# The values' products of two steps in one visit, in the last steps of an attention and MLP kernel

## The chip, the core and the metric

The kernel runs on one core of one Trainium2 chip. The metric is the device time of one execution in microseconds; three runs are shown by their median and their extremes. A profile was taken of one further execution: it has records of every instruction on the engines (PE for TensorE's matmuls, PEld for its weight loads, DVE for VectorE, ACT for ScalarE, POOL for GpSimd) and of the DMAs.

## The reference

An adaLN block over 2048 positions of width 512: attention with 32 heads of 16, then a dense layer to 1792, Mish, and a dense layer back.

```python
h = _layernorm(x) * (1 + ca) + sa
qkv = (h @ wqkv).reshape(B, S, 3, H, Dh)           # H = 32, Dh = 16
p = _softmax(einsum("bhqd,bhkd->bhqk", q, k) * Dh ** -0.5)
x = x + ga * (einsum("bhqk,bhkd->bhqd", p, v) @ wo)
h = _layernorm(x) * (1 + cb) + sb
x = x + gb * (mish(h @ w1 + b1) @ w2)              # all in float32
```

## The kernel before, in words

**Head groups and steps.** Attention is cut into 32 head groups `n`: four blocks of 512 queries (`qb`) times eight groups of four heads. A head group takes 16 steps, one for each 128 keys, so `T` is 512 steps, and the loop at the file's end calls `step(t)` one by one. Two steps, an even and an odd one, form a pair (`u`). In the even one PE makes the scores of the two heads that lie in rows 64 to 127, for two key chunks (four scores, `own`); in the odd one those of the two heads in rows 0 to 63. A score (L618) is a matmul with 64 rows by 512 queries into one of the `ring` banks of PSUM; ACT takes the exponential (L621) into a buffer `pr`. Each head has three or four such buffers.

**Maxima.** A softmax needs the maximum of every row ahead of its scores. DVE takes it, 20 steps (`PRO`) ahead of the scores, from a first pass of products (L569, L571). `tm = t + PRO`; from step 492 on `tm >= T`, and no maxima are left to make.

**The values' products.** `pv(t)` (L628 to L639) multiplies the exponentials of key chunk `t` with the values: four matmuls, one for each head, with 128 rows by 32 columns each, at four places of the array side by side, into the bank `acc`. In the trace each float32 matmul of this kind shows as two, so one `pv` shows as x8. I call it a visit, because scores and unit matmuls before and behind it use the array as two halves of 64 rows, and this one as four strips of 32 columns. `step(t)` calls `pv(t - 2)` once, at its end or, where the step has no unit matmuls and maxima are left, in its middle (`mid`).

**Units.** What is left over of PE beside the scores goes to the units: output projection, up and down matmuls of the MLP for the block of queries before. `next_part` takes up to eight matmuls of a unit for a pair of steps. `mm_half` runs each of them in two halves: in the even step with rows 0 to 63, beside the scores that use rows 64 to 127, and in the odd step the other way round. In the last 20 steps a part has six matmuls, and a whole unit of twelve takes two pairs. When its last half is issued, `cur["fin"]` empties the unit's only bank `ms` into SBUF: there DVE does it (L828 for an up unit, L1007 for a down unit), and the next unit writes to the same bank.

Both halves of a matmul write to one bank, and the two row halves must not do that at once. So the first half matmul of a step is made to wait for an instruction of the step before: after the last half of a part, `cur["want"]` is set, the step's fourth score is issued, and that score's exponential on ACT is kept in `cur["after"]`.

```python
        i = nc.tensor.matmul(acc, l[64 * g:64 * g + 64], r[64 * g:64 * g + 64], start=start and not then, stop=bool(stop and then))
        if after is not None:
            tc.add_manual_dep(i.ins, after.ins.name,
...
                for m in beside[i]:
                    mm_half(m, second, cur.pop("after", None))
                if last:
                    cur["want"] = True
                    if i < len(mine):
                        emit(mine[i])
```

(The lines from `mm_half`, L129 on, and from `step`, L1397 on.)

**The last steps.** From step 494 on `first_part` adds two matmuls per step of the last block's output projection (shown as L134 `ring<-ka,o_hl`), for which one bank of the six in the ring is kept. A step then has four scores and two of these in one row half, six unit matmuls in the other. Behind step 511 come two calls with `pv` alone, and then `tail()`, the MLP of the last block of queries.

The order on each engine is the order in which this code emits the instructions.

Of the kernel before, what the change touches and what calls it, by code (L numbers as in the profile page):

```python
# [18 lines left out]
def adaln_block(ctx: ExitStack, tc: tile.TileContext, x, wqkv, wo, w1, b1, w2, c, w_mod, out):  # L19
# [13 lines left out]
    T = 16 * NIT  # L33
# [126 lines left out]
    def bank(tag="ms"):  # L160
        return ring() if tag == "ring" else ps.tile([P, TB], F32, tag=tag, name="bk", bufs=1)
# [413 lines left out]
    def max_pair(n, jq, kb):  # L575

        if n not in mxs:
            mxs[n] = ap.tile([P, 2, 8, 4], F32, tag="mx", name="mx", bufs=2)
        j, qs = divmod(jq, 4)
        kt, qt = ka[(2 * n + j) % NR], qa[(2 * n + j) % NR]  # L580
        pm = ring(2)
        for s in range(2):
            nc.tensor.matmul(pm[:, s, :], qt[64 * s:64 * s + 64, qs * P:(qs + 1) * P],  # L583
                             kt[64 * s:64 * s + 64, kb * TB:(kb + 1) * TB], start=True, stop=True)
        nc.vector.tensor_reduce(out=mxs[n][:, :, jq, kb:kb + 1], in_=pm, op=ALU.max, axis=AX.X)

    def neg_max(n):

        mx = mxs.pop(n)
        mm = ap.tile([P, 4, 2, 4], F32, tag="mm", name="mm", bufs=2)  # L590
        for v in range(2):
            nc.vector.tensor_reduce(out=mm[:, :, v, :], in_=mx.rearrange("p s (j q) k -> p (s j) q k", j=2), op=ALU.max,
                                    axis=AX.X)
        ats.setdefault(16 * n + 16 - PRO, []).append(lambda: max_rows(n, mm))
# [19 lines left out]
    def score(n, j, s, kc):  # L614
        def product():
            kt, qt = ka[(2 * n + j) % NR], qa[(2 * n + j) % NR]
            p_ = ring()
            nc.tensor.matmul(p_, kt[64 * s:64 * s + 64, kc * P:(kc + 1) * P], qt[64 * s:64 * s + 64, :],  # L618
                             start=True, stop=True)
            pr = ap.tile([P, TB], F32, tag=f"p{2 * j + s}", name="pr", bufs=3 + s)  # L620
            e = nc.scalar.activation(pr, p_, AF.Exp, scale=SCALE)  # L621
            pts[16 * n + kc, 2 * j + s] = pr
            return e
        return product
# [3 lines left out]
    def pv(t):  # L628
        if not 0 <= t < T:
            return  # L630
        n, kc = divmod(t, 16)
        if kc == 0:
            accs[n] = bank("acc")
        for h in range(4):
            o = (kc * 4 + h) * VW
            nc.tensor.matmul(accs[n][32 * h:32 * h + 32, :], vgs[n][:, o:o + 32], pts.pop((t, h)),  # L636
                             start=(kc == 0), stop=(kc == 15))
        if kc == 15:
            evac(n)  # L639
# [651 lines left out]
    def whole_units(h, credit):  # L1291

        cur["owed"] = cur.get("owed", 0) + credit
        while cur["owed"] > 0.49:
            if not cur["left"]:
                if not units or h < units[0][0]():
                    cur["owed"] = 0
                    return
                cur["tag"] = "acc" if cur.get("tag") == "ms" else "ms"
                cur["fin"] = units.pop(0)[1](cur["tag"])  # L1300
                cur["left"] = list(pe_queue)
                pe_queue.clear()
            m = cur["left"].pop(0)
            mm_go(m)
            cur["owed"] -= m[0].shape[-1] / TB
            if not cur["left"]:
                at(h + 1, lambda fin=cur["fin"]: fin(h + 1))
                cur["fin"] = None

    def maxima(n, u, s, others):  # L1310

        j, qs = divmod(u, 4)
        return ([max_tile(n, j, s, qs, kb) for kb in range(4 - others)],
                [max_tile(n, j, 1 - s, qs, kb) for kb in range(4 - others, 4)])

    def step(t):
        second = t % 2
        n, u = t // 16, t % 16 // 2
        tm = t + PRO
        run_hooks(2 * t)  # L1320
        if t < 0:

            for i in range(2):
                if tm < 16:
                    kb, jq = divmod(2 * tm + i, 8)
                else:
                    jq, kb = tm % 16 // 2, 2 * second + i
                max_pair(tm // 16, jq, kb)
            if second and tm % 16 == 15:
                neg_max(tm // 16)  # L1330
            run_hooks(2 * t + 1)
            for f in ats.pop(t, []):
                f()
            whole_units(2 * t + 1, CREDIT)
            do_specials(2 * t + 1)
            return
        s = 0 if second else 1
        own, others = ([score(n, j, v, 2 * u + i) for i in range(2) for j in range(2)] for v in (s, 1 - s))
        if not second and t < T:
            next_part(2 * t)  # L1340
        part = list(cur["part"])
        if not second:
            first_of["part"] = []
            if t == T - PRO:
                kept.append(NRING - 1)
            elif T - PRO < t < T:
                first_part(2 * t)
        f = len(part)
        if t >= T:
            if t == T:  # L1350
                cur["tag"] = "acc"
            run_hooks(2 * t + 1)
            pv(t - 2)
            whole_units(2 * t + 1, 8)
            do_specials(2 * t + 1)
            return
        if tm < T:
            o = max(0, (8 - f) // 2)
            mo, alone = maxima(tm // 16, tm % 16 // 2, s, o)

            mine = [x for p in zip(mo, own) for x in p] + own[len(mo):]
        else:
            o = max(0, (4 - f) // 2)
            mine = own[o:] if second else own[:4 - o]
            alone = others[4 - o:] if second else others[:o]

            if first_of["part"]:
                assert f
                for i, slot in enumerate(first_of["part"]):
                    mine.insert(2 + 2 * i, lambda slot=slot: [mm_half(m, 1 - second, None, second) for m in slot] and None)  # L1370
            m = len(mine)
            if f > m:
                mine = [mine[(i * m) // f] if (i + 1) * m // f > i * m // f else None for i in range(f)]
        beside = part + alone

        def emit(product):
            e = product()
            if e is not None and cur.pop("want", None):
                cur["after"] = e

        mid = False
        if cur.pop("new", None) and alone and len(mine) > f and t % 16 != 2:

            emit(mine.pop())
            emit(beside.pop())
        for i in range(max(len(mine), len(beside))):
            if i == len(mine) // 2:
                run_hooks(2 * t + 1)

            if not f and tm < T and i == (2 if mst.get("norming") else 3):  # L1390
                pv(t - 2)
                mid = True
            if i < f:
                last = i + 1 == f
                if i < len(mine) and mine[i] and not last:
# [7 lines that stand above are left out]
                    if second and not cur["left"]:  # L1403
                        cur["fin"](2 * t + 2)
                        cur["fin"] = None
            else:
                for x in (*mine[i:i + 1], *beside[i:i + 1]):
                    emit(x)
        if second and first_of["part"] and not first_of["left"]:
            first_of["fin"]()  # L1410
        if tm < T and tm % 16 == 15:
            neg_max(tm // 16)
        do_specials(2 * t + 1)
        if not mid:
            pv(t - 2)
        for f in ats.pop(t, []):
            f()

    def do_specials(h):
        if specials and h >= specials[0][0]():  # L1420
            fin = specials.pop(0)[1]()
            pe_run()
            at(h + 1, lambda: fin(h + 1))
# [116 lines left out]
    def run_hooks(h):  # L1540
        for f in hooks.pop(h, []):
            f()

    for t in range(-PRO, T + 2):
        step(t)
        prep_step(t)
    t = T + 2
# [32 lines left out]
```

## Time and profile before

| | |
|---|---|
| median of three runs | 1690.04 us (1687.92 to 1691.31) |
| the profiled execution | 1688.32 us, of which the span is 1686.5 |
| PE, ACT, DVE, POOL busy in the span | 1670.4, 1357.4, 1432.9, 812.5 us |
| steps 492 to 511, with the visit that ends them | 54.40 us, from 1530.80 to 1585.20 |
| the granted clock there | 1.00 |

A timeline row gives start, duration, engine, line, operation, what is written from what, shape and count; like instructions in a row are merged, and the duration is then that of all of them together. In brackets stands idle time ahead of it and what ended it. A matmul's duration reaches from its start to the end of its pipeline, so matmuls of one row half overlap, and the distance of their starts is what one costs.

### The profile page before, as it was taken

To read this page: it belongs to the slowest core of one execution; us is meant where nothing else is said; L and a number is where in the kernel's file an instruction comes from. 1 tells how busy PE (TensorE), PEld (TensorE's weight loads), DVE (VectorE), ACT (ScalarE), POOL (GpSimd) and SP (SyncE) were. 2 spreads that over 40 slices of the span, in tenths; PEclk is the share of its full clock that TensorE was granted. 3 is DMA by queue.
4 is the path that set the end of the run, shared out by engine and by line. 5 is a ranking of instruction groups with operands and counts; after the bars stand their busy time and mean duration, and the time that the engine had idled before them with its cause. 6 is when DMAs were issued, how large, how long until landed. Compare 5 with 4: busy or idle time off the path is not lost.

```text
span 1686.5 us, 33920 instructions
## 1 busy us (share of the span) xinstructions
PE 1670.4 (99%) x12491; PEld 924.4 (55%) x12491; DVE 1432.9 (85%) x2372; ACT 1357.4 (80%) x2612; POOL 812.5 (48%) x839
## 2 busy tenths in 40 slices
PE   8999999999999999999999999999999999999998
PEld 6755655555445455555555455555555455555687
DVE  6998888888999988888889888888889888883377
ACT  7257777777778988888878998888878988889674
POOL 5555224655313664556323565556323664555442
PEclk9999999999999999999999999999999999999999
DMA  8877656777755334434355434534344433534261
GB/s 261 264 251 188 157 145 197 205 228 218 225 136 161 97 93 104 120 81 130 82 137 161 106 77 98 139 80 122 100 133 120 130 93 81 149 97 135 76 227 63
DMA packets 114983, 239.00 MB, mean 142 GB/s; under 512 B 24500, under 2 KB 50120, under 8 KB 108864
## 3 DMA queue, kind: packets, MB, share of 16 engines
q1 hardware_dynamic: 114808, 236.82, 49.7%
q8 instruction: 99, 1.62, 0.4%
q14 instruction: 68, 0.56, 0.1%
q10 hardware_dynamic: 8, 0.00, 0.0%
HBM read 180.48 MB, written 51.45 MB: 138 GB/s over the span
## 4 chain that ended last, share of the span: by engine, by line
PE 92%; DVE 3%; ACT 2%; DMA 1%; issue 1%; POOL 0%; SPq 0%; ACTq 0%; DVEq 0%; POOLq 0%
PE bk L636 29%; PE ring L618 22%; PE ring L569 19%; PE bk L134 11%; PE bk L127 3%; PE ring L127 2%; PE ring L1249 2%; DVE mx L571 2%; ACT pr L621 1%; PE ring L583 1%; DMA qa<-mt 0%; PE ring L952 0%; PE ring L598 0%; DMA xt<-in_A_x 0%; PE ring L134 0%
## 5 line engine op out<-in xcount | busy, mean ns | idle before, releaser
L571 DVE TENSOR_REDUCE mx<-ring 128x1 f32<-128x512 f32 x1968 | 1221.9, 681 | 150.9 <-PE ring L569 136.2
L621 ACT ACTIVATE pr<-ring 128x512 f32<-128x512 f32 x2048 | 1078.7, 603 | 207.8 <-PE bk L134 116.3
L569 PE MATMUL ring<-ka,qa 64*128 64x512 f32 x1968 | 818.3, 429 | 1.3 <-ACT pr L621 1.0
L618 PE MATMUL ring<-qa,ka 64*128 64x512 f32 x2048 | 759.0, 402 | 3.2 <-ACT pr L621 2.0
L636 PE MATMUL bk<-pr,vg 128*32 128x512 f32 x4096 | 545.1, 604 | 0.0
L569 PEld LDWEIGHTS ring<-ka,qa 64*128 64x128 f32 x1968 | 350.6, 184 | 326.4 <-DVE mx L571 251.4
L618 PEld LDWEIGHTS ring<-qa,ka 64*128 64x128 f32 x2048 | 373.6, 184 | 192.2 <-DVE mx L571 113.3
L134 PE MATMUL bk<-h,w 64*128 64x512 f32 (+1 forms) x1080 | 277.8, 390 | 0.0
L134 PE MATMUL bk<-w,a_h 64*128 64x512 f32 x632 | 210.8, 413 | 0.0
L134 PEld LDWEIGHTS bk<-h,w 64*128 64x128 f32 x1080 | 178.5, 184 | 9.2 <-ACT pr L621 1.5
L636 PEld LDWEIGHTS bk<-pr,vg 128*32 128x32 f32 x4096 | 81.2, 108 | 135.8 <-issue 126.5
L134 PE MATMUL bk<-w,a_l 64*128 64x512 f32 x316 | 124.0, 392 | 0.0
L134 PEld LDWEIGHTS bk<-w,a_h 64*128 64x128 f32 x632 | 106.7, 184 | 3.4 <-ACT hb L830 0.8
L1008 POOL TENSOR_TENSOR y<-yd,y 128x512 f32<-128x512 f32 x44 | 56.8, 1292 | 88.9 <-ACT yd L1007 79.5
L842 POOL TENSOR_SCALAR qq<-ee 128x512 f32<-128x512 f32 x25 | 15.5, 620 | 169.3 <-ACT ee L836 169.3
L858 POOL TENSOR_TENSOR qq<-qq,rr 128x512 f32<-128x512 f32 x42 | 54.1, 1289 | 85.8 <-ACT rr L852 85.8
L844 POOL TENSOR_TENSOR hb<-hb,ee 128x512 f32<-128x512 f32 x42 | 54.1, 1288 | 79.6 <-DVE ee L840 77.6
L134 PE MATMUL bk<-w,o_hl 64*128 64x512 f32 x288 | 79.3, 405 | 0.0
L96 POOL TENSOR_TENSOR a_l<-hb,a_h 128x512 fp32r<-128x512 f32 x53 | 73.1, 1379 | 4.4
L134 PEld LDWEIGHTS bk<-w,a_l 64*128 64x128 f32 x316 | 58.3, 184 | 2.8
L93 POOL TENSOR_SCALAR qh<-qf 128x512 fp32r<-128x512 f32 x27 | 16.7, 620 | 88.3 <-ACT qf L258 68.1
L134 PE MATMUL bk<-h_h,wl 64*128 64x512 f32 x168 | 57.3, 421 | 0.2 <-ACT pr L621 0.2
(222 smaller groups left out, 1901.3 us busy)
## 6 DMA issues: line engine op xcount, KB each, us to landing
ka<-kscr SPq DMA_DIRECT2D x124, 384.0 KB
w<-w2scr SPq DMA_DIRECT2D x56, 512.0 KB
w<-w1scr SPq DMA_DIRECT2D x46, 512.0 KB
vg<-vscr SPq DMA_DIRECT2D x32, 552.0 KB
qa<-qscr SPq DMA_DIRECT2D x124, 100.0 KB
kscr<-qh SPq DMA_DIRECT2D x16, 512.0 KB
qscr<-qh SPq DMA_DIRECT2D x32, 256.0 KB
w2scr<-hl SPq DMA_DIRECT2D x14, 512.0 KB
```

Source lines behind the costliest of these rows:

```text
L96: (nc.gpsimd if eng == "p" else nc.vector).tensor_sub(lo, src, hi.bitcast(F32))
L127: nc.tensor.matmul(acc, l, r, start=start, stop=stop)
L134: i = nc.tensor.matmul(acc, l[64 * g:64 * g + 64], r[64 * g:64 * g + 64], start=start and not then, stop=bool(stop and then))
L569: nc.tensor.matmul(pm, qt[64 * s:64 * s + 64, qs * P:(qs + 1) * P], kt[64 * s:64 * s + 64, kb * TB:(kb + 1) * TB], start=True, stop=True)
L571: nc.vector.tensor_reduce(out=mxs[n][:, s, 4 * j + qs, kb:kb + 1], in_=pm, op=ALU.max, axis=AX.X)
L618: nc.tensor.matmul(p_, kt[64 * s:64 * s + 64, kc * P:(kc + 1) * P], qt[64 * s:64 * s + 64, :], start=True, stop=True)
L621: e = nc.scalar.activation(pr, p_, AF.Exp, scale=SCALE)
L636: nc.tensor.matmul(accs[n][32 * h:32 * h + 32, :], vgs[n][:, o:o + 32], pts.pop((t, h)), start=(kc == 0), stop=(kc == 15))
L844: (nc.vector if tail else nc.gpsimd).tensor_mul(hb, hb, ee)
L858: nc.gpsimd.tensor_mul(qq, qq, rr)
L1008: nc.gpsimd.tensor_add(y[i], yd, y[i])
L1249: nc.tensor.matmul(po[i // 2][:, i % 2, :], l[:, s], w[:, r, :], start=(f == 0 and j == 0), stop=(f == FT - 1 and j == 2))
```

## The change

From step 492 on no visit is made at the end of a step (`mid` starts as true). In every odd step from 493 to 511 the products of two steps, `pv(t - 3)` and `pv(t - 2)`, are issued one after the other, ahead of the step's third score (`own[2]`). The visits of steps 510 and 511 come behind the loop's last step as before.

```diff
             o = max(0, (4 - f) // 2)
+            third = own[2]
             mine = own[o:] if second else own[:4 - o]
...
-        mid = False
+        mid = tm >= T
         if cur.pop("new", None) and alone and len(mine) > f and t % 16 != 2:
...
             if i == len(mine) // 2:
                 run_hooks(2 * t + 1)

+            if tm >= T and second and i < len(mine) and mine[i] is third:
+                pv(t - 3)
+                pv(t - 2)
             if not f and tm < T and i == (2 if mst.get("norming") else 3):
                 pv(t - 2)
                 mid = True
```

On PE, at the end of the even step 502 and in the odd step 503, this stood before (`qa_102` with `ka_700` and `qa_103` with `ka_701` are the scores of the two head pairs, `w_...,a_h` and `a_l` the unit's matmuls, `ka_702,o_hl` those of `first_part`; in brackets the engines whose work an instruction waits for):

```order
L134 MATMUL bk<-w_18213,a_l 128x512
L618 MATMUL ring<-qa_103,ka_701 128x512
L636 MATMUL bk<-pr,vg 32x512 x4
L618 MATMUL ring<-qa_102,ka_700 128x512
L134 MATMUL bk<-w_18174,a_h 128x512 [waits Activation_49]
L618 MATMUL ring<-qa_103,ka_701 128x512
L134 MATMUL bk<-w_18174,a_h 128x512
L134 MATMUL ring<-ka_702,o_hl 128x512
L134 MATMUL bk<-w_18174,a_l 128x512
L618 MATMUL ring<-qa_102,ka_700 128x512
```

and this stands there now:

```order
L134 MATMUL bk<-w_18213,a_l 128x512
L618 MATMUL ring<-qa_103,ka_701 128x512
L618 MATMUL ring<-qa_102,ka_700 128x512
L134 MATMUL bk<-w_18174,a_h 128x512 [waits Activation_49]
L618 MATMUL ring<-qa_103,ka_701 128x512
L134 MATMUL bk<-w_18174,a_h 128x512
L134 MATMUL ring<-ka_702,o_hl 128x512
L134 MATMUL bk<-w_18174,a_l 128x512
L636 MATMUL bk<-pr,vg 32x512 x8
L618 MATMUL ring<-qa_102,ka_700 128x512
```

The visit between the even step's fourth score and the odd step's first one is gone; the unit matmul that waits for ACT keeps its wait and now stands two instructions behind the fourth score, and eight value products stand ahead of the odd step's third score.

On PE from the odd step 505, in which a unit ends, to the even step 506, in which the next one starts, before:

```order
L134 MATMUL bk<-w_19295,a_l 128x512
L618 MATMUL ring<-qa_103,ka_701 128x512
L636 MATMUL bk<-pr,vg 32x512 x4
L618 MATMUL ring<-qa_102,ka_700 128x512
L134 MATMUL bk<-w_18174,a_h 128x512 [waits DVE_49]
L618 MATMUL ring<-qa_103,ka_701 128x512 [waits Activation_49]
```

and now:

```order
L134 MATMUL bk<-w_19295,a_l 128x512
L618 MATMUL ring<-qa_103,ka_701 128x512
L618 MATMUL ring<-qa_102,ka_700 128x512
L134 MATMUL bk<-w_18174,a_h 128x512 [waits DVE_49]
L618 MATMUL ring<-qa_103,ka_701 128x512 [waits Activation_49]
```

Here too the visit is gone from between the unit's last matmul and the next unit's first, which waits for DVE to have emptied the bank.

## The prediction

> **What bounds the kernel now.** I read the page first, then the busy times of the stretch that the change touches, then the timelines of TensorE (PE) and ScalarE (ACT) in it. The page says that PE is busy nearly all the time, and the stretch of the last twenty steps (492 to 511, from the end of step 491's visit to the first matmul of the closing part) says the same of itself:
>
> ```profile
> span 1686.5 us, 33920 instructions
> PE 1670.4 (99%) x12491; PEld 924.4 (55%) x12491; DVE 1432.9 (85%) x2372; ACT 1357.4 (80%) x2612; POOL 812.5 (48%) x839
> ...
> core 0: us, PE busy (x) PEld busy (x) DVE busy (x) ACT busy (x) POOL busy (x), PEclk, DMA share, GB/s
> 1530.80:1585.20 54.40, 54.40 (x417) 26.98 (x413) 8.56 (x16) 46.47 (x91) 32.02 (x30) 1.00 0.21 69
> ...
> 1585.20:1680.20 95.00, 95.00 (x450) 77.87 (x447) 72.44 (x101) 55.14 (x84) 34.98 (x38) 1.00 0.41 147
> ```
>
> PE is busy 54.40 of 54.40 us, at a granted clock of 1.00; ACT is busy 46.47. That would make every microsecond taken off PE a gain. The Trainium skill warns against that reading: "Trainium Kernel Development and Optimization", section Performance Expectations, says that matmul busy time is a bad metric since matmuls are pipelined. By the busy share the sum below would be its first term alone; the trace bears the warning out, since its rows of single matmuls show a second limit. In the PE timeline of two steps (L618 are scores, L134 `bk` unit matmuls, L134 `ring` those of the extra output units, L636 the values' products):
>
> ```profile
> 1547.91 0.39 PE L618 MATMUL ring<-qa,ka 64*128 64x512 f32 x1
> 1547.97 0.40 PE L134 MATMUL bk<-h,w 64*128 64x512 f32 x1
> 1548.30 1.07 PE L636 MATMUL bk<-pr,vg 128*32 128x512 f32 x8
> 1549.30 0.49 PE L618 MATMUL ring<-qa,ka 64*128 64x512 f32 x1
> 1549.39 0.50 PE L134 MATMUL bk<-h,w 64*128 64x512 f32 x1
> 1549.63 0.39 PE L618 MATMUL ring<-qa,ka 64*128 64x512 f32 x1
> ...
> 1550.42 0.39 PE L134 MATMUL bk<-h,w 64*128 64x512 f32 x1
> 1550.56 0.39 PE L618 MATMUL ring<-qa,ka 64*128 64x512 f32 x1
> 1550.65 0.40 PE L134 MATMUL bk<-h,w 64*128 64x512 f32 x1
> 1550.98 1.06 PE L636 MATMUL bk<-pr,vg 128*32 128x512 f32 x8
> 1551.97 0.49 PE L618 MATMUL ring<-qa,ka 64*128 64x512 f32 x1
> 1551.98 0.49 PE L134 MATMUL bk<-h,w 64*128 64x512 f32 x1
> ...
> 1554.56 0.49 PE L618 MATMUL ring<-qa,ka 64*128 64x512 f32 x1
> 1554.62 0.50 PE L134 MATMUL bk<-h,w 64*128 64x512 f32 x1
> ```
>
> and the ACT timeline of the same time, where L621 x4 are a step's four exponentials:
>
> ```profile
> 1547.26 2.07 ACT L621 ACTIVATE pr<-ring 128x512 f32<-128x512 f32 x4
> 1549.18 0.66 ACT L852 ACTIVATE rr<-rr 128x512 f32<-128x512 f32 x1
> 1549.83 2.06 ACT L621 ACTIVATE pr<-ring 128x512 f32<-128x512 f32 x4
> 1552.51 2.06 ACT L621 ACTIVATE pr<-ring 128x512 f32<-128x512 f32 x4 [0.61 <-PE ring L618]
> ```
>
> A step's first unit matmul waits for the exponential of the step before's fourth score. That exponential ends at 1547.26 + 2.07 = 1549.33, 1551.89 and 1554.57; the unit matmul starts at 1549.39, 1551.98 and 1554.62. In the first and third case it starts 0.05 to 0.06 us after the exponential's end and 0.09 and 0.06 us behind the score ahead of it, which the visit had released: the wait is the last to end, by a hair. The visit of 1.00 us at the step's end is what covers it.
>
> **What the change saves.** From the last unit matmul to a visit 0.33 us (1547.97 to 1548.30), the visit 1.00 (to 1549.30), the next score 0.33 later, where matmuls of one row half otherwise follow each other every 0.23 (1550.42 to 1550.65). A visit thus takes 0.33 + 1.00 + 0.33 - 2 x 0.23 = 1.20 us of PE. The last visit of the stretch runs three steps' products together and so shows what a further step in the same visit costs:
>
> ```profile
> 1582.17 0.39 PE L134 MATMUL bk<-w,a_l 64*128 64x512 f32 x1
> 1582.49 2.78 PE L636 MATMUL bk<-pr,vg 128*32 128x512 f32 x24
> 1585.20 0.96 PE L1138 MATMUL bk<-ka,o_hl 128*128 128x512 f32 x3
> ```
>
> 2.71 us against 1.00 is 0.86 for each step more (1.71 / 2). Before, there are 19 single visits and the triple one; now 11 double ones (steps 493, 495 ... 511 and the closing one). Nine visits fewer, each worth 1.20 - 0.86 = 0.34: **-3.1 us**. Its ends are 0 (if a second step costs a full visit's price again) and -3.1.
>
> The transpose of line 598 at the end of step 492 loses the visit that it stood behind:
>
> ```profile
> 1532.37 1.07 PE L636 MATMUL bk<-pr,vg 128*32 128x512 f32 x8
> 1533.37 0.28 PE L598 MATMUL ring<-ident,mm 128*32 128x128 f32 x1
> 1533.58 0.50 PE L134 MATMUL bk<-h,w 64*128 64x512 f32 x1
> ```
>
> There it took 0.21 us; alone it may take up to 0.33 more, but stands where PE waits anyway (next part): 0, ends 0 and +0.3.
>
> **What it uncovers, from an even step to the odd one.** Ten step ends (492 to 510) have no visit any more, and the next step's first unit matmul stands two instructions behind the fourth score. From that score's start: 0.39 to its end, 0.04 until ACT starts (1549.30 + 0.49 = 1549.79, exponential at 1549.83), 0.61 for the exponential (a row of four takes 2.06, and the mean below is 605 ns), 0.05 back to PE: 1.09 us at the least.
>
> ```profile
> L621 ACT ACTIVATE pr<-ring 128x512 f32<-128x512 f32 x81 | 41.9, 605 | 5.9 <-PE ring L618 5.3 <-PE bk L134 0.4
> ```
>
> The unit matmul would otherwise come 0.23 after the last one, and that can lie up to 0.2 behind the fourth score (the delayed first unit matmul of the even step now goes beside the second score, so six unit matmuls stand against five of the other row half). That leaves 1.09 - 0.43 = 0.66 of waiting; after a pause the next pair comes at 0.33 instead of 0.23: 0.76. The other end is today's distance: the exponential of the score at 1550.56 ended at 1551.89, 1.33 later, because ACT worked through four in a row; with it 1.33 + 0.05 - 0.43 + 0.10 = 1.05. I take 0.80, close to the lower end, since in the new order PE's pause ahead of the second score lets ACT catch up. **10 x 0.80 = +8.0 us** (7.6 to 10.5). I count with all that stands behind the waiting matmul on PE waiting too, so that scores, and with them ACT, stand still.
>
> **From an odd step to the even one** (nine ends, 493 to 509). The double visit ends at V. Third score at V, its exponential at V + 0.54 (1551.97 to 1552.51), the fourth score's one 0.49 later ((2.06 - 0.61) / 3), done at V + 1.64, PE goes on at V + 1.69. The last three unit matmuls stand at V, V + 0.33, V + 0.56, the next is due at V + 0.79. Waiting 0.90, with the restart 1.00. At five of the nine ends a unit has also finished (493, 497, 501, 505, 509), and DVE must first empty its bank:
>
> ```profile
> 1535.35 0.75 DVE L828 TENSOR_SCALAR hb<-bk,b1c 128x512 f32<-128x512 f32 x1 [1.02 <-PE bk L134]
> 1545.83 0.69 DVE L1007 COPY yd<-bk 128x512 f32<-128x512 f32 x1 [3.06 <-PE bk L134]
> ...
> 1545.32 0.40 PE L134 MATMUL bk<-w,a_l 64*128 64x512 f32 x1
> ```
>
> The unit's last matmul ended at 1545.72 and DVE began at 1545.83, 0.11 later. So V + 0.56 + 0.40 + 0.11 + 0.69 (or 0.75) + 0.05 = V + 1.81 (1.87), a wait of 1.02 to 1.08, with the restart 1.15. **4 x 1.00 + 5 x 1.15 = +9.7 us** (8 to 11).
>
> **Small terms.** The waits of 0.09, 0.01 and 0.06 seen above go, 18 times 0.05: -0.9. ACT's other work (0.66 at 1549.18) now fits beside the double visit where it stands at the start of an odd step; two pieces stand at the start of an even one (steps 496 and 504) and delay its exponentials by some 0.5 each: +1.0. Together 0. SP, POOL and the DMAs keep their order; buffers of `pr` suffice, since a visit frees two of them per head ahead of the third score. ACT's copy of head group 30's sums moves half a step forward, beside the visit: 0. The closing part behind 1585.20 has PE busy in all of its 95.00 us up to 1680.20 (the last row of the first fence), so a delay passes through to the end.
>
> **Sum:** -3.1 + 8.0 + 9.7 + 0 = **+14.6 us**, or 1.53 per two steps. Against the profiled execution's 1688.32 us (span 1686.5 and 1.8 around it) that is 1702.9; the median of the runs shown is 1.7 higher, 1690.04, so I forecast **1704.6 us**.
>
> **Rivals.** *All waits stay covered.* Then only the first term is left: 1686.9 us, faster. For it speaks that PE shows 54.40 of 54.40 us and that ACT, at 46.5, would still fit into 51.3. Against it: the fourth score's exponential would have to end within 0.43 us of the score's start, and one exponential alone takes 0.61. That is also where it decides. Chance 0.05. The Trainium skill would lead to it: "TensorEngine Tiling (Array Packing)", section Key Properties, says that a change of tiling mode drains the array, so fewer changes pay; the 1.20 and 0.86 above agree with that, but it says nothing of what the drained time covers.
>
> *Only one kind of boundary pays*, because the pause at the one lets ACT run ahead for the other: -3.1 + 9.7 = +6.6 or -3.1 + 8.0 = +4.9, 1695 to 1697 us. For it: the pauses do give ACT time. Against: both waits start from a score that PE has only just issued. Chance 0.08.
>
> *The waits are longer*, both at their upper ends, because ACT works off four exponentials in a row as today and its two extra pieces come on top: 10.5 + 11 - 3.1 + 1.0 = +19.4, 1709.4 us. Chance 0.07: PE's pauses thin out ACT's queue.
>
> That nothing measurable happens needs gains and waits to cancel; between the first two rivals, 0.02. That the order is not changed as described is ruled out by the instruction order itself.
>
> **How the numbers follow.** The forecast, 1700 to 1708, has 0.78. The range 1697 to 1710 takes in the upper edge of the second rival and most of the third, and the bounds of both waits; it leaves out some 0.15. A measurement tells about 0.2% (3.4 us) from no change: faster 0.05, same 0.02, slower 0.93.
>
> **What would show it.** L636 in runs of sixteen, about 1.86 us from start to the next score; two steps take some 6.8 us instead of 5.3; ahead of a step's first unit matmul PE waits for `pr` of L621 (14 times, 0.7 to 1.0 us) and for L828 or L1007 on DVE (five times, about 1.1); the stretch grows from 54.4 to about 69 us while ACT's busy time stays near 46. I am wrong if PE shows no waits there, or if they are half as long.

## The result, and the profile after

The changed kernel is slower: 1705.27 us (median of five runs, 1704.31 to 1708.2) against 1690.0, a ratio of 1.0095 with a 95% interval of 1.0081 to 1.011. The forecast was 1704.6 us. The profiled execution took 1705.34 us, 17.0 more than that of before. Its page, and the busy times of the last twenty steps and of 95 us of the closing part (first number after the stretch: its length, then PE, PEld, DVE, ACT, POOL busy, the clock, the DMA share and GB/s):

```profile
span 1703.5 us, 33920 instructions
PE 1675.9 (98%) x12491; PEld 926.8 (54%) x12491; DVE 1434.1 (84%) x2372; ACT 1359.2 (80%) x2612; POOL 812.6 (48%) x839
...
1531.36:1602.22 70.86, 59.87 (x417) 28.55 (x413) 8.54 (x16) 47.61 (x90) 31.54 (x30) 1.00 0.17 53
...
1602.22:1697.22 95.00, 95.00 (x450) 77.87 (x447) 72.45 (x101) 55.13 (x84) 35.36 (x39) 1.00 0.41 147
```

The stretch has grown from 54.40 to 70.86 us, by 16.5; the closing part has not changed. Each engine has as many instructions in it as before, within one, and PE is no longer busy all the time: 59.87 of 70.86 us. Where it stands still is seen in its timeline, from the end of step 496 to the start of step 499:

```profile
1546.84 0.39 PE L134 MATMUL bk<-w,a_l 64*128 64x512 f32 x1
1547.07 0.39 PE L618 MATMUL ring<-qa,ka 64*128 64x512 f32 x1
1548.07 0.50 PE L134 MATMUL bk<-w,a_h 64*128 64x512 f32 x1 [0.61 <-ACT pr L621]
...
1548.65 0.39 PE L134 MATMUL bk<-w,a_l 64*128 64x512 f32 x1
1548.97 1.93 PE L636 MATMUL bk<-pr,vg 128*32 128x512 f32 x16
1550.83 0.50 PE L618 MATMUL ring<-qa,ka 64*128 64x512 f32 x1
...
1551.40 0.39 PE L134 MATMUL bk<-w,a_l 64*128 64x512 f32 x1
1551.63 0.39 PE L618 MATMUL ring<-qa,ka 64*128 64x512 f32 x1
1552.74 0.47 PE L134 MATMUL bk<-h,w 64*128 64x512 f32 x1 [0.71 <-DVE yd L1007]
...
1553.77 0.39 PE L618 MATMUL ring<-qa,ka 64*128 64x512 f32 x1
1553.97 0.39 PE L134 MATMUL bk<-h,w 64*128 64x512 f32 x1
1554.20 0.39 PE L618 MATMUL ring<-qa,ka 64*128 64x512 f32 x1
1555.06 0.50 PE L134 MATMUL bk<-h,w 64*128 64x512 f32 x1 [0.46 <-ACT pr L621]
```

The double visit costs what it should: 1548.97 to 1550.83, 1.86 us. But at every step end that lost its visit, the next unit matmul starts 1.1 to 1.4 us after the last one instead of 0.23. In these rows it is once released by an exponential, once by DVE's emptying of the unit's bank (1552.74), once by an exponential again. The view of waits, for PE and its weight loads in this stretch (in total, how often, the longest), names the same two:

```profile
PEld bk L134 <- ACT pr L621: 16.6, 17, 1.1
PE bk L134 <- ACT pr L621: 8.3, 15, 0.8
PE bk L134 <- DVE hb L828: 1.4, 2, 0.7
PE bk L134 <- DVE yd L1007: 1.3, 2, 0.7
```

In the view of before only the first of these pairs is there at all:

```profile
PEld bk L134 <- ACT pr L621: 0.8, 1, 0.8
```

### The profile page after: what moved, and what is told of

It reads as the page before. It is cut to its first block, busy times and chain, and to the rows that moved or that the text cites. A ratio compares the mean times of both kernels' runs of the same rounds, so it can differ in the third digit from the quotient of the medians.

```text
span 1703.5 us, 33920 instructions
## 1 busy us (share of the span) xinstructions
PE 1675.9 (98%) x12491; PEld 926.8 (54%) x12491; DVE 1434.1 (84%) x2372; ACT 1359.2 (80%) x2612; POOL 812.6 (48%) x839
## 4 chain that ended last, share of the span: by engine, by line
PE 89%; ACT 3%; DVE 3%; DMA 3%; issue 1%; POOL 0%; SPq 0%; ACTq 0%; DVEq 0%
PE bk L636 29%; PE ring L618 21%; PE ring L569 19%; PE bk L134 12%; ACT pr L621 2%; PE ring L127 2%; PE ring L1249 2%; PE bk L127 2%; DVE mx L571 2%; DMA w1scr<-ep 1%; DMA qa<-mt 0%; PE ring L952 0%; PE ring L598 0%; DMA qscr<-qh 0%; DMA xt<-in_A_x 0%
## 5 line engine op out<-in xcount | busy, mean ns | idle before, releaser
L621 ACT ACTIVATE pr<-ring 128x512 f32<-128x512 f32 x2048 | 1080.2, 603 | 222.5 <-PE bk L134 117.8
L134 PE MATMUL bk<-h,w 64*128 64x512 f32 (+1 forms) x1080 | 278.9, 391 | 3.0 <-ACT pr L621 2.3
L134 PE MATMUL bk<-w,a_h 64*128 64x512 f32 x632 | 211.5, 414 | 8.0 <-ACT pr L621 6.0
L134 PEld LDWEIGHTS bk<-h,w 64*128 64x128 f32 x1080 | 178.2, 184 | 13.8 <-ACT pr L621 6.4
L134 PE MATMUL bk<-w,a_l 64*128 64x512 f32 x316 | 124.2, 393 | 0.0
L134 PEld LDWEIGHTS bk<-w,a_h 64*128 64x128 f32 x632 | 106.2, 184 | 17.7 <-ACT pr L621 10.8
L134 PE MATMUL bk<-w,o_hl 64*128 64x512 f32 x288 | 79.3, 405 | 0.0
L134 PEld LDWEIGHTS bk<-w,a_l 64*128 64x128 f32 x316 | 58.3, 184 | 3.6
L134 PE MATMUL bk<-h_h,wl 64*128 64x512 f32 x168 | 57.4, 421 | 0.2 <-ACT pr L621 0.2
```

## The experiments

Theory: the step ends without a visit show two waits that the visits had covered. Rival: the long visits themselves do it, since PE makes no scores for 1.86 us, ACT runs dry, and everything behind it comes late. The ACT timeline of the changed kernel speaks for it (in brackets the idle time ahead):

```profile
1558.41 3.93 ACT L621 ACTIVATE pr<-ring 128x512 f32<-128x512 f32 x7 [1.91 <-PE ring L618]
```

The experiments move the visits without merging them, merge them at other places, and change the wait while the visits stay.

The figures below are medians; those of the first four stand against 1689.27 us of the kernel before on the same chip, those of the last three against 1688.59.

**Moved, not merged.** The changed kernel with one visit of one step in every step:

```diff
-            if tm >= T and second and i < len(mine) and mine[i] is third:
-                pv(t - 3)
+            if tm >= T and i < len(mine) and mine[i] is third:
                 pv(t - 2)
```

> The visits move but are not merged: from step 492 on every step makes its one visit ahead of its third score, so that both kinds of step end lose their visit as in the changed kernel, and no visit is saved (20 single ones and a double one, where the kernel before has 19 and a triple one). Theory of the uncovered waits: from the profile after, ten even-to-odd ends cost 10.3 us and nine odd-to-even ends 10.1, the old small waits of 0.9 go and one visit more costs 0.3: 1690.0 + 19.8 = 1709.8 us, slower than the changed kernel by 3.4 (its nine merged visits and one). Rival, that the long blocks of 1.85 us starve ACT of scores: the blocks are 1.0 us again, so at most half of the loss is left, below 1698 us.

Measured: 1706.97 us, ratio 1.0102 (1.0086 to 1.0118), +17.7. The stretch:

```profile
1529.63:1603.54 73.91, 63.28 (x417) 26.46 (x414) 8.55 (x16) 47.93 (x91) 31.55 (x30) 1.00 0.15 51
```

73.91 us is 3.05 more than with merged visits (70.86), where 3.4 were expected of ten visits more. So merging saves what the first term of the prediction says, and the whole loss is there without it. The stretch is 19.5 us longer than before, where 19.8 were expected; the median is 2.8 us below the expected 1709.8. With visits no longer than before, the rival had at most half of the loss left.

**Only the even steps' visit moved.** In the odd step the first product runs ahead of the third score, the second at the step's end:

```diff
-        mid = tm >= T
+        mid = tm >= T and not second
...
                 pv(t - 3)
-                pv(t - 2)
```

> Only the even steps' visit is moved: in an odd step the first product runs ahead of the third score and the second one at the step's end, as before. Unmerged, and only the ten even-to-odd ends are uncovered. Theory of the uncovered waits: 10.3 - 0.5 = +9.8, 1699.8 us. Rival (blocks that starve ACT): blocks of 1.0 us as before, near 1690, at most 1693 us.

Measured: 1701.45 us, ratio 1.0068 (1.0053 to 1.0082), +12.2. The stretch, and PE at an uncovered end:

```profile
1530.59:1596.77 66.18, 58.47 (x418) 25.53 (x414) 8.54 (x16) 47.01 (x90) 31.91 (x30) 1.00 0.17 57
...
1557.70 0.39 PE L134 MATMUL bk<-h,w 64*128 64x512 f32 x1
1557.70 0.62 PE L618 MATMUL ring<-qa,ka 64*128 64x512 f32 x2
1559.09 0.50 PE L134 MATMUL bk<-h,w 64*128 64x512 f32 x1 [0.76 <-ACT pr L621]
```

Visits of one step each, nothing merged, and still 12 us more: the rival's 1693 us is out of reach. It is 2 us above what the theory gave, since each end costs 1.39 us here (1557.70 to 1559.09) and not 1.1: behind a visit at the step's start ACT works off four exponentials in a row. 10 x (1.39 - 0.23 + 0.10) - 0.5 = 12.1.

**Merged at the end of the even steps.** The same eleven double visits, but standing where an even step ends:

```diff
         if not mid:
             pv(t - 2)
+        elif tm >= T and not second:
+            pv(t - 2)
+            pv(t - 1)
```

(and the two calls ahead of the third score taken out).

> The same merging, eleven double visits, but at the end of the even steps, so that only the nine odd-to-even ends are uncovered. Theory of the uncovered waits: -3.1 + 10.1 - 0.5 = +6.5, 1696.5 us. Rival (blocks that starve ACT): the blocks are as long as in the changed kernel, so about as slow, 1703 to 1706 us.

Measured: 1698.49 us, ratio 1.0048 (1.0032 to 1.0063), +9.2.

```profile
1532.60:1595.70 63.10, 55.46 (x417) 27.67 (x413) 8.54 (x16) 47.26 (x90) 31.82 (x30) 1.00 0.18 60
...
1556.54 0.39 PE L134 MATMUL bk<-h,w 64*128 64x512 f32 x1
1556.77 0.38 PE L618 MATMUL ring<-qa,ka 64*128 64x512 f32 x1
1557.92 0.49 PE L134 MATMUL bk<-h,w 64*128 64x512 f32 x1 [0.77 <-ACT pr L621]
```

The visits are as long as in the changed kernel, and the stretch is 7.8 us shorter: their place counts, not their length. The expected 1696.5 us is missed by 2, again because the ends are longer, 13.3 us in sum where the changed kernel's nine take 11.25. At seven of them the exponential is what PE waits for last: six take 1.38 to 1.54 us (here 1556.54 to 1557.92), and one, where ACT's copy of a head group's sums and a piece of a unit come ahead of the step's exponentials, 2.08.

**The wait changed, a first try.** From step 492 on the next unit matmul waits for a copy of one column of the fourth score by DVE, instead of for the exponential (cut here: the tile `tok`, and the line that keeps the score's bank):

```diff
             if e is not None and cur.pop("want", None):
-                cur["after"] = e
+                cur["after"] = e if tm < T else nc.vector.tensor_copy(tok, cur["bank"][:, :1])
```

> The changed kernel, but from step 492 on a step's first unit matmul waits for a copy of one column of the fourth score by the idle DVE instead of that score's exponential on ACT. The order it keeps is the same. From the last unit matmul: 0.39 + 0.11 + about 0.16 (the mean of the smallest DVE pieces) + 0.05 = 0.71 us instead of 1.09 to 1.16, so 0.4 less at ten even-to-odd ends and at the four odd-to-even ends where no unit ends; at the other five DVE's emptying comes about 0.1 later. Theory of the uncovered waits: 1705.3 - 5.6 + 0.5 = 1700.2 us. Rival (blocks that starve ACT): the visits stay where they are, so no gain, 1704 to 1706 us.

Measured: 1714.42 us, ratio 1.0143 (1.0126 to 1.016): slower than the changed kernel instead of faster. The copy stood behind the exponential in the program and reads the same bank, and the profile has it waiting for ACT (a row of the waits) and starting only as the exponential ends. (Lines added to the file shift the numbers in this run and the next ones: L135 here is L134 above, L622 is L621.)

```profile
DVE tok L1382 <- ACT pr L622: 67.7, 20, 6.0
...
1548.92 0.40 PE L135 MATMUL bk<-w,a_l 64*128 64x512 f32 x1
...
1550.23 0.49 PE L135 MATMUL bk<-w,a_h 64*128 64x512 f32 x1 [0.69 <-DVE tok L1382]
```

So the wait was lengthened, not shortened: 1.31 us from unit matmul to unit matmul instead of 1.09, and about 2.0 instead of 1.3 where DVE's emptying came behind the copy. The expectation was wrong on what the edit does; the run shows that a longer wait makes a slower kernel. The rival, which gives no change here, does not fit either. (A part of its time has another cause, told in the last section.)

**The wait shortened.** The same copy, issued ahead of the exponential (the tile `tok` is cut here too):

```diff
+            if cur.pop("token", None):
+                cur["after"] = nc.vector.tensor_copy(tok, p_[:, :1])
             e = nc.scalar.activation(pr, p_, AF.Exp, scale=SCALE)
...
-                    cur["want"] = True
+                    cur["want" if tm < T else "token"] = True
```

> The changed kernel, with the wait really shortened: from step 492 on DVE copies one column of the step's fourth score ahead of that score's exponential (not behind it), and the next step's first unit matmul waits for that copy. From the last unit matmul 0.39 + 0.11 + 0.16 + 0.05 = 0.71 us (the copy took 0.16 us in the kernel with the late copy) instead of 1.09 to 1.30, at ten even-to-odd ends and four odd-to-even ends: 14 x 0.42 = 5.9 less; where a unit ends, DVE's emptying comes 0.1 to 0.2 later, 5 x 0.15 = 0.7 more. Theory of the uncovered waits: the stretch of the last twenty steps 70.9 - 5.2 = 65.7 us, the time about 5 us below the changed kernel's, 1700 us. Rival (long blocks that starve ACT): the visits stand where they stood, no gain, 1704 to 1706 us.

Measured: 1698.96 us, ratio 1.0061 (1.0047 to 1.0074), +10.4 where the changed kernel has +15.3.

```profile
1529.13:1593.65 64.52, 60.13 (x417) 28.39 (x413) 10.89 (x36) 47.84 (x91) 31.65 (x30) 1.00 0.18 58
...
1555.63 0.39 PE L135 MATMUL bk<-h,w 64*128 64x512 f32 x1
1555.87 0.39 PE L619 MATMUL ring<-qa,ka 64*128 64x512 f32 x1
1556.31 0.50 PE L135 MATMUL bk<-h,w 64*128 64x512 f32 x1
```

0.68 us from 1555.63 to 1556.31 (0.71 was expected), and the stretch falls from 70.86 to 64.52 us (65.7 expected). The visits stand exactly where they stood, as long as they were, and ACT still pauses behind them, for up to 1.72 us; only the wait is shorter. That decides against the rival, by which nothing was to be gained.

**The same copy in the kernel before.**

> The kernel before with the same earlier copy. Its step ends are covered by visits, so only the small waits go (0.09, 0.01, 0.06 us in its rows, some 0.9 us in all). Theory of the uncovered waits: stretch 53.5 us instead of 54.4, the time 0.9 us less, which is too little to tell. Rival that the wait for the exponential costs the kernel before as much as the changed one: about 5 us less.

Measured: 1687.27 us, ratio 0.9992 (0.9983 to 1.0001): no difference that the runs can tell.

```profile
1530.44:1584.25 53.81, 53.81 (x418) 25.04 (x414) 11.08 (x36) 46.20 (x91) 32.04 (x30) 1.00 0.22 70
```

The stretch is 0.6 us shorter than 54.40. The shorter wait is worth 6.3 us where it is uncovered and 0.6 where visits cover it.

**And in the kernel with double visits at the even steps' ends.**

> Double visits at the end of the even steps, with the earlier copy. Only the nine odd-to-even ends are uncovered; the four without a unit's end fall from about 1.4 to 0.71 us, the five with one stay near 1.4. Theory of the uncovered waits: stretch 63.1 - 4 x 0.7 = 60.3 us, 1695.7 us, between the kernel before and the same kernel with the late wait. If the copy lets DVE's emptying alone remain, no merging of visits at these places pays, since five ends still cost about 6 us against the 3.1 saved.

Measured: 1694.01 us, ratio 1.003 (1.0019 to 1.0042), +5.4.

```profile
1532.15:1591.47 59.32, 55.64 (x417) 27.82 (x413) 10.90 (x36) 46.70 (x90) 31.81 (x30) 1.00 0.20 63
```

The best of the merged versions is still slower than before: five ends remain at which DVE empties a unit's bank (1.28 to 1.34 us each), and they cost more than the 3.1 us that merging saves. What these five ends cost is read from the rows: no run took DVE's emptying away by itself. No version here beats the kernel before by more than the runs can tell.

## Why the prediction was right, point by point

- **What bounds the kernel.** Right: PE's busy share of 100% hid a second limit, and the wait behind it showed as soon as the visits had moved.
- **The saving of nine visits, -3.1 us.** Right: the double visit lasts 1.86 us as worked out from the triple one, and the unmerged version is 3.05 us longer. It makes ten visits more, and its nineteen ends take 22.5 us against 22.9; that leaves 0.35 us for each visit, where 0.34 was forecast.
- **Even to odd, +8.0 us.** Too small by 2.3. The ten ends take 11.6 us from last to next unit matmul in the timeline; less 10 x 0.23, with 10 x 0.10 for the restart, 10.3 us. At three ends ACT is late. At steps 496 and 504 its extra pieces delay it (ends of 1.23 and 1.30 instead of 1.09, together some 0.35; the prediction had 1.0 for them among the small terms). At step 492 the end takes 1.42, since the visit that still closes step 491 stands ahead of the step's scores, and ACT then works off four exponentials in a row, up to 1533.98:

```profile
1531.92 2.06 ACT L621 ACTIVATE pr<-ring 128x512 f32<-128x512 f32 x4 [0.56 <-PE ring L618]
1534.04 0.50 PE L134 MATMUL bk<-h,w 64*128 64x512 f32 x1 [0.81 <-ACT pr L621]
```

  That is the queue behind the prediction's upper bound for this term, and it came at one end of ten. The transpose of line 598 stands inside this wait and adds nothing to it, as the prediction had it. At the other seven ends (1.09 to 1.11) the step that was off is the credit of "up to 0.2" because the fourth score starts ahead of the last unit matmul. It does (1553.77 against 1553.97), but its exponential does not start 0.04 after the score's end at 1554.16. It starts at 1554.41, 0.05 after the end of the unit matmul that precedes the score in the program (0.05 to 0.07 at all seven):

```profile
1554.41 0.60 ACT L621 ACTIVATE pr<-ring 128x512 f32<-128x512 f32 x1
```

  ACT itself was not what held it back: with exponentials waiting it starts one 0.49 us after the other (1551.44 and 1551.93), and here the one before had started 0.64 earlier. So the 1.09 us count from the last unit matmul, and the credit is void: 1.09 - 0.23 + 0.10 = 0.96 for each end instead of the 0.80 taken. That the later matmul's end is only signalled behind the earlier one's is what these rows suggest; no run took it apart.
- **Odd to even, +9.7 us.** Right: 11.25 us in nine ends, less 2.07, with 0.9 for the restarts, 10.1. Ends without a unit's end take 1.16 to 1.25 us (worked out: 1.69 - 0.56 = 1.13), those with one 1.25 to 1.34 (1.25 to 1.31).
- **Small terms, 0.** The old waits of 0.9 went; the extra pieces of ACT cost less than the 1.0 set against them.
- **Sum.** -3.1 + 10.3 + 10.1 - 0.9 = 16.4 against 16.5 measured in the stretch (70.86 - 54.40), where 14.6 had been forecast. The medians differ by 15.3; the profiled executions by 17.0, of which 0.5 lie ahead of the stretch. That the forecast came within 0.7 us of the median is in part luck: the stretch grew by 1.9 us more than forecast, and the medians differ by 1.2 us less than the stretches do.
- **Rivals.** That all waits stay covered, and that only one kind of end pays, both fell: the waits stand at all nineteen ends, and moving either kind alone costs 12.2 us (even to odd, unmerged) or 9.2 (odd to even, merged). The third, that both waits are at their upper ends, came close in the first (10.3 against 10.5) and not in the second (10.1 against 11). Its reason, four exponentials in a row, held at the end of step 492 alone; with only the even steps' visit moved it does hold, and the ends take 1.39 us.
- **What would show it.** The visits come in runs of sixteen, 1.86 us long, and two steps take about 7.0 us (1548.97 to 1555.96) where 6.8 were named. The brackets of the rows, 0.46 to 0.81 us, look shorter than the waits of 0.7 to 1.0 and 1.1 that were named. They count from the end of the last matmul in PE's pipeline, the prediction from when the next unit matmul was due, 0.23 after the last one; by that count the waits are 0.86 to 1.19, those at a unit's end 1.02 to 1.11.

## What to carry to other kernels

Work that does not wait for anything may be covering a wait, and then its place is worth more than its price: before moving such a block, look at what is released just as it ends. Here the sign was in four rows of the timeline, a matmul that started 0.05 us after an exponential's end while its engine showed 100% busy. A saving on PE can be counted only as far as the round trip through the other engine is shorter than what stays in between.

## What the runs showed that was not expected

In the kernel with the late copy, the granted clock of PE fell inside the stretch (in the second piece, from 1537 us on; the clock is the third number from the end):

```profile
1532.00:1537.00 5.00, 3.95 (x27) 1.56 (x27) 0.64 (x4) 2.44 (x6) 4.75 (x5) 1.00 0.13 25
1537.00:1544.00 7.00, 5.77 (x25) 3.17 (x29) 0.85 (x3) 3.80 (x7) 0.02 (x1) 0.57 0.15 59
...
1537.74 0.65 PE L135 MATMUL bk<-w,a_h 64*128 64x512 f32 x1 [1.57 <-DVE hb L830]
1538.19 0.62 PE L135 MATMUL bk<-w,a_h 64*128 64x512 f32 x1
1538.62 0.62 PE L135 MATMUL bk<-w,a_l 64*128 64x512 f32 x1
```

Matmuls then follow each other every 0.43 us instead of 0.23. The clock fell about at the end of a pause of 1.57 us, with another of 1.02 us some 5 us earlier; single pauses of up to 1.38 us later in the same stretch left it at 1.00, and so did one of 1.45 us in the kernel with double visits at the even steps' ends. The Trainium skill, "TensorE: Matmul & The Clock Gate", section HAM oscillation, ties a halved clock to idle gaps of over some 3.4 us; the longest pause here was less than half of that, so by that rule the clock should have stayed. In the 3.4 us ahead of the fall PE was busy for 1.83 us; in the emptiest 3.4 us around the pause of 1.45 us it was busy for 1.95. Whether the length of one pause or the idle time of several decides was not tried. The granted clock over that profiled execution of 1711.98 us was 0.997 against 0.999 in the changed kernel. From the start of step 494 to the end of the double visit behind it the execution takes 7.97 us (1537.74 to 1545.71) and the changed kernel 5.12 (1538.66 to 1543.78). The longer wait accounts for 0.2 of the difference, so some 2.6 us belong to the clock and not to the wait; without them it would still be the slower kernel.
